# Fifteen-product block multiply over 512 tokens, in-place quarter sums, and one held PSUM bank

## The chip, the cores and the metric

The kernel runs on one core of one Trainium2 chip. The metric is device time in microseconds of one execution. The engines are named as in the profile: PE is TensorE (PEld its weight loads), DVE is VectorE, ACT is ScalarE, POOL is GpSimd, SP is the engine whose queue issues most of the transfers.

## The reference

An attention block (a linear recurrence with decay, per head) feeds a token and channel mixer. There are 4 batches, 768 tokens and 8 heads of 48, so 384 channels. All is float32.

```python
for t in range(S):                                   # attention, per batch and head
    y[t] = r[t] @ (state + outer(u * k[t], v[t]))
    state = w[t][:, None] * state + outer(k[t], v[t])
x = y, laid out as (batch, token, 384)
h = relu(x.T @ w_tok1) @ w_tok2                      # w_tok1 (768, 256), w_tok2 (256, 768)
u = x + h.T
out = u + relu(u @ w_ch1) @ w_ch2                    # w_ch1 (384, 1536), w_ch2 (1536, 384)
```

The weights arrive as 64-bit floats in their bits and are converted on the chip.

## The kernel before, in words

The attention is cut into 12 units of 256 tokens, three to a batch. While a batch is mixed, the three units of the next batch run beside it; the last batch is mixed alone. The first batch is mixed with plain matmuls, since the weights are still being converted and combined beside it.

A middle batch is written by `middle_mixing` as a list of pieces, each a cost weight and a function that issues instructions. `woven` merges lists: every piece gets the position of its middle in its list, as a fraction of the list's total weight, and the pieces are sorted by that. `strict` then makes each of PE, DVE and ACT issue its instructions in exactly the order of the merged list, so an instruction that waits holds all that stand behind it on its engine. Transfers of SP are not held to the list's order.

The mixing of a batch has these stages.

- `hidden`: the first token product, two results of 6 matmul calls each, with 384 columns. A float32 matmul call shows as two instructions in the profile.
- `back` and `turn`: six times the second token product, which DVE adds to x (L531), and three transposes into `xT`, copied by ACT (L538).
- The up projection to `z` (1536 hidden values for each token), in three segments of 256 tokens. For the batches after the first it is a block multiply with fifteen products in place of eighteen. `rights(s)` makes sums of blocks of `xT` on DVE (L569, L499), named g, h, f, e, r12, r13, r9, r0, r4, r7, r2, r10; the matching sums of `w_ch1` are made once. `thirds(s)` issues fifteen products (L582). A product is four matmul calls of 128 columns into one PSUM bank. After it come its taps: "take" is an ACT copy to `z` (L587), "plus", "minus" and "rest" are DVE adds (L590, L593, L596), and "done" is the Relu on ACT in place (L599). The numbers 14, 8, 12, 9, ... are the products' order.
- The down projection, again in three segments: `quarters(s)` splits `z` into a11, a12, a21, a22 and uses seven products p1 to p7 in place of eight. Each is two halves of three matmul calls with 192 columns (L639, L643). DVE makes four sums of quarters (L686, L687) and taps the products into the output tile `o`, of which there is one; p1 is copied by ACT to m1, and m1, u2 and u3 are running sums in SBUF (L652, L669, L675). SP stores `o` in two parts (L647).

In a middle batch each segment goes through `thirds` and then `quarters`. All middle segments use the second `z` buffer; the sums of the quarters lie in the first. Of the attention units, `ends` is a scan on DVE (L372) with a memset ahead and a reciprocal behind, `keys`, `begins` (a second scan, L380) and `queries` follow it, `tokens` transposes keys on PE, `gram`, `carry`, `before` and `after` are small PE matmuls, and `products` are three DVE operations that prepare the diagonal of a later unit. `load_rk` and its like are SP's transfers.

Eight PSUM banks: two for `carry`'s result, six in a pool `ps_m` that everything else takes in turn.

```python
keyed.append(((at + c / 2) / total, n, i, c, f))            # woven
pieces = woven(hiddens + turned[:6] + sums[:3] + ... , a0 + a1 + a2 + b0)
for s, (att, near) in enumerate(((b1, n + 1), (b2 + c0, n + 2), (c1 + c2, n + 3))):
```

Here a, b and c are the three units of the next batch: part 0 is the loads and `ends`, part 1 goes from `keys` to the first updates, part 2 from `gram` to the copies of the result.

Of the kernel before, what the change touches and what calls it, by code (L numbers as in the profile page):

```python
# [62 lines left out]
def rwkv6_then_mixer(  # L63
# [48 lines left out]

    rks = [const.tile([128, 2 * COLS], f32, name=f"rk{i}") for i in range(3)]
# [75 lines left out]
    early = [t.bitcast(u32) for t in halves]  # L189
    bits64 = [t[:, :4 * PIECE] for t in (scratch, spare, early[0])]  # L190
# [284 lines left out]
    z_sums = [halves[0][:, ts(i, HJ * 128)].rearrange("p (j t) -> p j t", j=HJ) for i in range(3)]  # L475
    w_sums = [scratch[:, ts(i, HJ * HM)].bitcast(f32).rearrange("p (j e) -> p j e", j=HJ) for i in range(3)]
    parts = halves[0][:, ds(3 * HJ * 128, 3 * HM)].rearrange("p (n e) -> p n e", n=3)
    late_sums = [t.rearrange("p q x t -> p (q x t)")[:, :HJ * 128].rearrange("p (j t) -> p j t", j=HJ) for t in ats]
    late_sums.append(starts[:, :HJ * 128].rearrange("p (j t) -> p j t", j=HJ))
    late_parts = ws[0][:, :3 * HM].rearrange("p (n e) -> p n e", n=3)  # L480
# [32 lines left out]
    def mixing(bt, x_of, out_rows):  # L513
# [5 lines left out]
        def hidden(i, c):  # L519
            if c == 0:  # L520
                sums[i] = ps_m.tile([128, DM], f32, name="h1_ps", tag="m")
            pe.matmul(sums[i], wtok1[:, c, ts(i, 128)], x_of()[:, c, :], start=(c == 0), stop=(c == C - 1))  # L522
            if c == C - 1:
                act.activation(h1[:, i, :], sums.pop(i), AF.Relu)  # L524
# [15 lines left out]
        def up(s, jt):  # L540
            if jt == 0:
                zs[s] = halves[int((bt, s) != (0, 0))].rearrange("p (j t) -> p j t", j=NJ)
            ps = ps_m.tile([128, SEG], f32, name="z_ps", tag="m")
            for m in range(DM // 128):
                pe.matmul(ps, wch1[:, m, ts(jt, 128)], xT[:, m, ts(s, SEG)],  # L545
                          start=(m == 0), stop=(m == DM // 128 - 1))
            act.activation(zs[s][:, jt, :], ps, AF.Relu)

        def rights(s):
            b = lambda k, m: xT[:, k, ds(s * SEG + m * 128, 128)]  # L550
            if not last:
                four = h1.rearrange("p i e -> p (i e)")[:, :512] if s % 2 else rights_at[:, 8 * 128:]
                eight = rights_at[:, :8 * 128]
            elif s % 2 == 0:
                near = apool.tile([128, 12 * 128], f32, name="near", bufs=1)
                four, eight = near[:, :512], near[:, 512:]
            else:
                eight, four = apool.tile([128, 8 * 128], f32, name="to_end"), apool.tile([128, 4 * 128], f32, name="kT", bufs=1)
            h, f, e, g = (four[:, ts(n, 128)] for n in range(4))
            r12, r13, r9, r0, r4, r7, r2, r10 = (eight[:, ts(n, 128)] for n in range(8))  # L560
            of = {0: r0, 1: b(0, 1), 2: r2, 3: b(0, 0), 4: r4, 5: f, 6: b(2, 1), 7: r7, 8: b(1, 0), 9: r9, 10: r10, 11: e,
                  12: r12, 13: r13, 14: g}
            hfe = four[:, :3 * 128].rearrange("p (k t) -> p k t", k=3)
            first, second = (xT[:, :, ds(s * SEG + m * 128, 128)] for m in range(2))
            sums = ((dve.tensor_add, g, b(0, 1), b(1, 1)), (dve.tensor_add, hfe, first, second), (dve.tensor_sub, r12, b(0, 0), e),
                    (dve.tensor_sub, r13, b(0, 0), b(2, 0)), (dve.tensor_add, r9, r13, g), (dve.tensor_sub, r0, b(2, 1), b(1, 0)),
                    (dve.tensor_add, r4, f, h), (dve.tensor_sub, r7, h, e), (less, r2, b(1, 1), b(2, 1)),
                    (dve.tensor_add, r10, b(1, 0), b(2, 0)))
            return of, [(0.05, lambda q=q: q[0](*q[1:])) for q in sums]  # L569

        def thirds(s, of):
            z = halves[s % 2 if last else 1].rearrange("p (j t) -> p j t", j=NJ)
            to = lambda n: z[:, ts(n // 2, JB), ts(n % 2, 128)]
            banks = {}

            def product(r, name, end):
                first = name not in banks
                if first:
                    banks[name] = bank("z_ps").rearrange("p (q t) -> p q t", q=JB)
                ps = banks[name]  # L580
                for q in range(JB):
                    pe.matmul(ps[:, q], lefts[r][:, ts(q, 128)], of[r], start=first and q == 0, stop=end and q == JB - 1,  # L582
                              skip_group_check=True)
                return ps

            def take(n, ps):
                act.copy(to(n), ps)  # L587

            def plus(n, ps):
                dve.tensor_add(to(n), to(n), ps)  # L590

            def minus(n, ps):
                dve.tensor_sub(to(n), to(n), ps)  # L593

            def rest(n, ps):
                dve.tensor_sub(to(n), ps, to(n))  # L596

            def done(n, ps):
                act.activation(to(n), to(n), AF.Relu)  # L599

            order = ((14, "x", False, [(take, 3)]), (8, "y", False, [(take, 2)]), (12, "z", False, [(take, 4)]),
                     (9, "x", False, [(plus, 2)]), (0, "y", False, [(minus, 4)]), (4, "u", False, [(take, 0)]),
                     (13, "x", True, [(minus, 0), (take, 1)]), (5, "y", False, [(take, 5)]), (6, "v", False, [(plus, 5)]),
                     (7, "z", True, [(plus, 1)]), (2, "y", True, [(plus, 3), (done, 3)]), (10, "u", True, [(rest, 2), (done, 2)]),
                     (3, "w", True, [(minus, 0), (minus, 4), (done, 0)]), (1, "q", True, [(plus, 5), (plus, 1), (done, 5), (done, 1)]),
                     (11, "v", True, [(minus, 4), (done, 4)]))

            def one(r, name, end, taps):
                ps = product(r, name, end)
                for f, n in taps:  # L610
                    f(n, ps)

            return [(0.9, lambda q=q: one(*q)) for q in order]
# [14 lines left out]
        def quarters(s):  # L628
            z = halves[s % 2 if last else 1].rearrange("p (j t) -> p j t", j=NJ)
            a11, a12, a21, a22 = (z[:, ts(j, HJ), ts(i, 128)] for i in range(2) for j in range(2))  # L630
            s1, s2, s4 = late_sums if last else z_sums
            t1, t2, t4 = w_sums
            m1, u2, u3 = ((late_parts if last else parts)[:, i] for i in range(3))
            L = {}

            def begin(a, b):
                L["q"] = ps_m.tile([128, HM], f32, name="q_ps", tag="m")
                for j in range(HJ // 2):
                    pe.matmul(L["q"], a[:, j, :], b[:, j, :], start=(j == 0), stop=False)  # L639

            def product(a, b):
                for j in range(HJ // 2, HJ):
                    pe.matmul(L["q"], a[:, j, :], b[:, j, :], start=False, stop=(j == HJ - 1))  # L643
                return L.pop("q")
# [4 lines left out]
            def p1():  # L649
                o = L["o"] = mpool.tile([128, 2, DM], f32, name="o", bufs=1)  # L650
                x = L["x"] = x_of()[:, ts(s, 2), :]
                act.copy(m1, product(a11, w11))  # L652
                dve.tensor_add(o[:, 0, :HM], x[:, 0, :HM], m1)

            def p4():
                o, x = L["o"], L["x"]
                dve.tensor_add(o[:, 1, :HM], x[:, 1, :HM], product(a22, t4))

            def p2():
                o = L["o"]  # L660
                dve.tensor_add(o[:, 0, :HM], o[:, 0, :HM], product(a12, w21))

            def p5():
                o, x = L["o"], L["x"]
                dve.tensor_add(o[:, :, HM:], x[:, :, HM:], product(s1, t1).unsqueeze(1).to_broadcast([128, 2, HM]))

            def p6():
                o = L["o"]
                dve.tensor_add(u2, m1, product(s2, t2))  # L669
                dve.tensor_add(o[:, 0, HM:], o[:, 0, HM:], u2)  # L670

            def p7():
                o = L["o"]
                both = o[:, 1].rearrange("p (n e) -> p n e", n=2)
                dve.tensor_add(u3, u2, product(a21, w12))  # L675
                dve.tensor_add(both, both, u3.unsqueeze(1).to_broadcast([128, 2, HM]))
                store(1)

            def p3():
                o = L["o"]  # L680
                dve.tensor_add(o[:, 0, HM:], o[:, 0, HM:], product(s4, w22))
                store(0)

            of = {p1: (a11, w11), p4: (a22, t4), p2: (a12, w21), p5: (s1, t1), p6: (s2, t2), p7: (a21, w12), p3: (s4, w22)}
            ps = {p: [(0.98, lambda p=p: begin(*of[p])), (0.98, p)] for p in of}
            return [*ps[p1], (0.01, lambda: dve.tensor_add(s1, a21, a22)), *ps[p4], (0.01, lambda: dve.tensor_sub(s2, s1, a11)), *ps[p2],  # L686
                    (0.01, lambda: dve.tensor_sub(a21, a11, a21)), *ps[p5], (0.01, lambda: dve.tensor_sub(s4, a12, s2)), *ps[p6], *ps[p7],  # L687
# [265 lines left out]
```

## Time and profile before

| | us |
|---|---|
| median of 3 runs | 518.55 (518.52 to 519.9) |
| the profiled execution | 518.99 |
| its span, first to last instruction | 517.3 |
| outside the span | 1.7 |
| first batch and the opening | 0 to 176.9 |
| second batch | 176.9 to 294.85 |
| third batch | 294.85 to 412.77 |
| last batch | 412.77 to 517.3 |

| engine | busy us | share | instructions |
|---|---|---|---|
| PE | 491.1 | 95% | 5794 |
| PEld | 428.4 | 83% | 5794 |
| DVE | 388.7 | 75% | 633 |
| ACT | 229.6 | 44% | 533 |

The ends of matmuls are modelled in the profile: a matmul of 192 columns shows 0.33 us, but in a stream the next one starts 0.16 us after it. So a pause of PE under about 0.2 us shows as busy, and a longer one shows shorter than it is. In a timeline a row gives the start, the length, the engine, the line and the operation; several equal instructions in a row are merged, and brackets give the idle time ahead and what ended it. "Hand-over" below is the moment at which PE could start the next matmul.

### The profile page before, as it was taken

To read this page: it belongs to the slowest core of one execution; us is meant where nothing else is said; L and a number is where in the kernel's file an instruction comes from. 1 tells how busy PE (TensorE), PEld (TensorE's weight loads), DVE (VectorE), ACT (ScalarE), POOL (GpSimd) and SP (SyncE) were. 2 spreads that over 40 slices of the span, in tenths; PEclk is the share of its full clock that TensorE was granted. 3 is DMA by queue.
4 is the path that set the end of the run, shared out by engine and by line. 5 is a ranking of instruction groups with operands and counts; after the bars stand their busy time and mean duration, and the time that the engine had idled before them with its cause. 6 is when DMAs were issued, how large, how long until landed. Compare 5 with 4: busy or idle time off the path is not lost.

```text
span 517.3 us, 13323 instructions
## 1 busy us (share of the span) xinstructions
PE 491.1 (95%) x5794; PEld 428.4 (83%) x5794; DVE 388.7 (75%) x633; ACT 229.6 (44%) x533; POOL 1.3 (0%) x10
## 2 busy tenths in 40 slices
PE   3678999999999999999999999999999999999996
PEld 2566588666789768999999868999999859999996
DVE  7999779959896878977779668987858616684653
ACT  2868665464353436434325445524335414531300
POOL 0000000000000000000000000000000000000000
PEclk9799999999999999999999999999999999999999
DMA  8856845442342442121211522100000000000000
GB/s 298 314 179 190 246 162 163 158 145 99 109 119 80 147 132 64 63 74 63 70 55 62 165 74 63 61 32 1 3 32 1 18 15 1 1 2 34 1 32 34
DMA packets 20945, 46.06 MB, mean 89 GB/s; under 512 B 2128, under 2 KB 13008, under 8 KB 20880
## 3 DMA queue, kind: packets, MB, share of 16 engines
q1 hardware_dynamic: 20736, 45.14, 27.3%
q8 instruction: 47, 0.77, 0.6%
q14 instruction: 18, 0.15, 0.1%
q10 hardware_dynamic: 144, 0.00, 0.0%
HBM read 40.41 MB, written 4.72 MB: 87 GB/s over the span
## 4 chain that ended last, share of the span: by engine, by line
PE 71%; DVE 17%; ACT 6%; issue 3%; DMA 2%; SPq 0%; DVEq 0%; ACTq 0%
PE z_ps L582 18%; PE q_ps L643 12%; PE q_ps L639 11%; PE h_ps L529 5%; PE h_ps L621 5%; PE h_ps L522 5%; PE z_ps L545 3%; PE y_ps L317 2%; PE gram L257 2%; DVE w L380 2%; PE y_ps L338 2%; PE kv_ps L303 2%; PE xT_ps L537 2%; DVE z L590 2%; DVE to_end L372 1%
## 5 line engine op out<-in xcount | busy, mean ns | idle before, releaser
L438 ACT ACTIVATE before<-state,to_end 112x48 f32<-112x48 f32 x176 | 44.5, 325 | 66.4 <-DVE state L448 62.5
L587 ACT COPY z<-z_ps 128x512 f32<-128x512 f32 x54 | 30.6, 587 | 57.4 <-PE z_ps L582 39.5
L590 DVE TENSOR_TENSOR z<-z,z_ps 128x512 f32<-128x512 f32 x54 | 36.0, 684 | 24.5 <-PE z_ps L582 15.9
L545 PE MATMUL z_ps<-xT,wch 128*128 128x256 f32 x216 | 48.1, 381 | 0.0
L599 ACT ACTIVATE z<-z 128x512 f32<-128x512 f32 x54 | 33.3, 631 | 33.1 <-DVE z L590 29.0
L545 PEld LDWEIGHTS z_ps<-xT,wch 128*128 128x128 f32 x216 | 40.6, 190 | 6.0 <-DVE wch L227 0.3
L643 PE MATMUL q_ps<-wch,z 128*128 128x192 f32 x222 | 43.3, 331 | 0.0
L639 PE MATMUL q_ps<-wch,z 128*128 128x192 f32 x222 | 42.8, 329 | 0.2
L639 PEld LDWEIGHTS q_ps<-wch,z 128*128 128x128 f32 x222 | 36.5, 190 | 0.9 <-ACT z L599 0.6
L643 PEld LDWEIGHTS q_ps<-wch,z 128*128 128x128 f32 x222 | 36.5, 190 | 0.6
L529 PE MATMUL h_ps<-h,wtok 128*128 128x384 f32 x96 | 35.1, 492 | 0.6 <-ACT h L524 0.6
L593 DVE TENSOR_TENSOR z<-z,z_ps 128x512 f32<-128x512 f32 x45 | 30.1, 685 | 6.9 <-PE z_ps L582 6.5
L621 PE MATMUL h_ps<-wch,z 128*128 128x384 f32 x96 | 33.3, 494 | 0.4 <-DVE wch L227 0.4
L522 PE MATMUL h_ps<-x,wtok 128*128 128x384 f32 x96 | 33.1, 491 | 0.0
L531 DVE TENSOR_TENSOR x<-x,h_ps 128x384 f32<-128x384 f32 x24 | 13.3, 553 | 26.1 <-PE h_ps L529 26.1
L582 PE MATMUL z_ps<-rk,wch 128*128 128x128 f32 x256 | 31.2, 275 | 0.0
L582 PEld LDWEIGHTS z_ps<-rk,wch 128*128 128x128 f32 x256 | 30.0, 192 | 0.0
L372 DVE TENSOR_TENSOR_SCAN to_end<-w,starts 112x1041 f32<-112x1041 f32 (+1 forms) x13 | 28.1, 2160 | 2.1 <-DMA w<-in_w_dram 1.7
L380 DVE TENSOR_TENSOR_SCAN w<-w,starts 112x1041 f32<-112x1041 f32 x12 | 27.9, 2322 | 0.0
L643 PE MATMUL q_ps<-scratch,z 128*128 128x192 f32 x144 | 27.7, 329 | 0.0
L639 PE MATMUL q_ps<-scratch,z 128*128 128x192 f32 x144 | 27.4, 327 | 0.0
L582 PE MATMUL z_ps<-xT,wch 128*128 128x128 f32 x216 | 27.1, 275 | 0.0
(181 smaller groups left out, 905.9 us busy)
## 6 DMA issues: line engine op xcount, KB each, us to landing
rk<-in_rk_dram SPq DMA_DIRECT2D x36, 192.0 KB, 3.8
near<-in_near_dram SPq DMA_DIRECT2D x8, 768.0 KB, 4.4
w<-in_w_dram SPq DMA_DIRECT2D x11, 520.5 KB, 4.2
vt<-in_v_dram SPq DMA_DIRECT2D x12, 384.0 KB, 4.0
out_dram<-o SPq DMA_DIRECT2D x24, 192.0 KB, 1.9
spare<-in_w_ch_dram SPq DMA_DIRECT2D x8, 512.0 KB, 4.3
scratch<-in_w_ch_dram SPq DMA_DIRECT2D x8, 512.0 KB, 4.7
rk<-in_rk_dram SPq DMA_DIRECT2D x6, 512.0 KB, 8.9
```

Of the source, the lines that this page charges most:

```text
L372: dve.tensor_tensor_scan(to, of, start, 0.0, op0=ALU.mult, op1=ALU.add)
L380: dve.tensor_tensor_scan(w_[:ROWS], w_[:ROWS], starts[:ROWS], 0.0, op0=ALU.mult, op1=ALU.add)
L438: act.mul(t[:ROWS, a], state[bt, g][:ROWS, a], by_last(c, j)[:, a:a + 1])
L522: pe.matmul(sums[i], wtok1[:, c, ts(i, 128)], x_of()[:, c, :], start=(c == 0), stop=(c == C - 1))
L529: pe.matmul(ps, wtok2[:, i, ts(c, 128)], h1[:, i, :], start=(i == 0), stop=(i == DTOK // 128 - 1))
L545: pe.matmul(ps, wch1[:, m, ts(jt, 128)], xT[:, m, ts(s, SEG)], start=(m == 0), stop=(m == DM // 128 - 1))
L582: pe.matmul(ps[:, q], lefts[r][:, ts(q, 128)], of[r], start=first and q == 0, stop=end and q == JB - 1, skip_group_check=True)
L590: dve.tensor_add(to(n), to(n), ps)
L599: act.activation(to(n), to(n), AF.Relu)
L621: pe.matmul(ps, zs[s][:, jt, ts(n, 128)], wch2[:, jt, :], start=(jt == 0), stop=(jt == NJ - 1))
L639: pe.matmul(L["q"], a[:, j, :], b[:, j, :], start=(j == 0), stop=False)
L643: pe.matmul(L["q"], a[:, j, :], b[:, j, :], start=False, stop=(j == HJ - 1))
```

## The change

The first two segments are multiplied together. With `s == 0`, `rights` and `thirds` work on 512 tokens: every block of `xT` is 256 tokens wide, and the fifteen products run twice, each with two matmul calls of 256 columns, for the first and then for the second two of each four blocks of hidden values. `z` of the first segment lies in buffer 0, of the second in buffer 1, of the third in buffer 0 again. Product 8 is issued ahead of product 14. The sum e is made alone, and three sums are written over their inputs (h, and two blocks of `xT`).

In `quarters` the sums are written over a22, a21, a11 and a12, each after the product that reads the old content. The products come in the order p4, p1, p2, p5, p6, p3, p7. p1, p6 and p7 add into one PSUM bank, tapped three times: m1, u2 and u3 are gone. That bank comes from a pool of one, `held`, which `ps_m` (now five) gives up; product bank "v" of `thirds` and the first `hidden` result of the batches after the first use it too.

A middle batch is now: hidden, back and turn; `thirds` of two segments; quarters 0; `thirds` of the third segment; quarters 1; quarters 2. The products for unit n+3 move from the third `thirds` to quarters 2. The last two turns go between the first products. In the last batch the check of the ranges (`verdict`) moves ahead of quarters 0.

```diff
+    def held(name):
+        return ps_h.tile([128, 512], f32, name=name, tag="h")
...
+    def z_of(s):
+        return halves[s % 2].rearrange("p (j t) -> p j t", j=NJ)
...
-                sums[i] = ps_m.tile([128, DM], f32, name="h1_ps", tag="m")
+                sums[i] = (held if bt and i == 0 else bank)("h1_ps")[:, :DM]
...
+            width = SEG if s == 0 else SEG // 2
...
+            b = lambda k, m: xT[:, k, ds(s * SEG + m * width, width)]
+            g, e, r12, r13, h, f = (six[:, ts(n, width)] for n in range(6))
+            r9, r0, r4 = (three[:, ts(n, width)] for n in range(3))
...
+            sums = ((dve.tensor_sub, r13, b(0, 0), b(2, 0)), (dve.tensor_add, g, b(0, 1), b(1, 1)), (dve.tensor_add, e, b(2, 0), b(2, 1)),
+                    (dve.tensor_sub, r12, b(0, 0), e), (dve.tensor_add, r9, r13, g), (dve.tensor_sub, r0, b(2, 1), b(1, 0)),
+                    (dve.tensor_add, hf, first, second), (dve.tensor_add, r4, f, h), (dve.tensor_sub, h, h, e),
+                    (less, b(1, 1), b(1, 1), b(2, 1)), (dve.tensor_add, b(2, 0), b(1, 0), b(2, 0)))
...
+            by_half = s == 0
+            count = JB // 2 if by_half else JB
+            order = ((8, "y", False, [("take", 2)]), (14, "x", False, [("take", 3)]), (12, "z", False, [("take", 4)]),
+                     (9, "x", False, [("plus", 2)]), (0, "y", False, [("minus", 4)]), (4, "u", False, [("take", 0)]),
...
+                     (1, "q", True, [("plus", 5), ("plus", 1), ("done", 5), ("done", 1)]), (11, "v", True, [("minus", 4), ("done", 4)]))
+
+            def to(n, at):
+                z = z_of(n % 2 if by_half else s)[:, ds(n // 2 * JB + at, count), :]
+                return z if by_half else z[:, :, ts(n % 2, 128)]
...
+                    banks[name] = (held if name == "v" else bank)("z_ps").rearrange("p (q t) -> p q t", q=count)
...
-                for q in range(JB):
-                    pe.matmul(ps[:, q], lefts[r][:, ts(q, 128)], of[r], start=first and q == 0, stop=end and q == JB - 1,
+                for q in range(count):
+                    pe.matmul(ps[:, q], lefts[r][:, ts(at + q, 128)], of[r], start=first and q == 0, stop=end and q == count - 1,
...
+            chain = (p1, p6, p7)
+
+            def begin(p, a, b):
+                if p in chain[1:]:
+                    L[p] = L[chain[0]]
+                else:
+                    L[p] = (held if p in chain else bank)("q_ps")[:, :HM]
+                half(0, L[p], a, b, first=p not in chain[1:])
...
+            of = {p1: (a11, w11), p4: (a22, t4), p2: (a12, w21), p5: (a22, t1), p6: (a11, t2), p7: (a21, w12), p3: (a12, w22)}
...
+            return [*ps[p4], (0.01, lambda: dve.tensor_add(a22, a21, a22)), *ps[p1], (0.01, lambda: dve.tensor_sub(a21, a11, a21)),
+                    (0.01, lambda: dve.tensor_sub(a11, a22, a11)), *ps[p2], (0.01, lambda: dve.tensor_sub(a12, a12, a11)), *ps[p5], *ps[p6],
+                    *ps[p3], *ps[p7]]
...
-    ps_g, ps_m = None, six_banks.enter_context(tc.tile_pool(name="ps_m", bufs=6, space=bass.MemoryType.PSUM))
+    ps_m, ps_h = (six_banks.enter_context(tc.tile_pool(name=name, bufs=n, space=bass.MemoryType.PSUM)) for name, n in (("ps_m", 5), ("ps_h", 1)))
...
+    def begun(turned, sums):
+        return turned[:5] + sums[:1] + turned[5:9] + sums[1:3] + turned[9:10] + sums[3:]
+
+    def with_turned(turned, ups):
+        return ups[:1] + turned[10:11] + ups[1:2] + turned[11:] + ups[2:]
...
+        pieces = woven([e for h in hiddens for e in h] + begun(turned, sums), a0 + a1 + a2 + b0)
+        ups = with_turned(turned, thirds(0, of))
+        pieces += ups[:4] + woven(ups[4:20], products_of(n + 1)) + ups[20:]
+        of, sums = rights(2)
+        pieces += woven(b1, woven(quarters(0), sums))
+        ups = thirds(2, of)
+        pieces += ups[:1] + woven(ups[1:11], products_of(n + 2)) + ups[11:]
+        pieces += woven(b2 + c0, quarters(1)) + woven(products_of(n + 3) + c1 + c2, quarters(2))
```

## The prediction

> **What bounds the kernel now.** I read the page's busy table and slices first, then the waits of TensorE in windows, then the chain for the price of a matmul, then timelines at the places the change touches.
>
> ```profile
> PE 491.1 (95%) x5794; PEld 428.4 (83%) x5794; DVE 388.7 (75%) x633; ACT 229.6 (44%) x533; POOL 1.3 (0%) x10
> PE   3678999999999999999999999999999999999996
> PEclk9799999999999999999999999999999999999999
> ```
>
> From a fifth of the span on TensorE is full, at full clock. The waits of PE in 294.85 to 412.77 us (the whole third batch) are one line:
>
> ```profile
> PE gram L257 <- DVE rk L383: 0.2, 1, 0.2
> ```
>
> So no wait of TensorE is left to take away there; a gain has to come out of its stream, and each new wait is paid in full. The chain gives the stream's prices:
>
> ```profile
> 139.06 5.38 PE z_ps L545 x24
> 145.51 2.79 PE z_ps L545 x12
> 319.98 11.61 PE z_ps L582 x104
> 412.77 7.74 PE h_ps L522 x24
> ```
>
> 5.38 - 2.79 over twelve is 215.8 ns for 256 columns, 11.61/104 is 111.6 ns for 128, 7.74/24 is 322.5 ns for 384; the chain's q_ps pieces (0.97 for six) give 162.5 for 192. Every product call is two instructions.
>
> **Stream.** In each of the last three batches 240 matmuls of 128 columns become 120 of 256: 26.79 - 25.90 = 0.9 us, three batches **-2.7**. The Trainium skill ("TensorE: Matmul & The Clock Gate", Back-to-back issue gap) puts a fixed 2.5 ns on a matmul beside its columns; 360 fewer would by that save 0.9 us in all. The rows show 2 x 111.6 - 215.8 = 7.4 ns a pair, so I take 2.7. The stream of the quarters keeps its 84 matmuls each.
>
> **Work taken off VectorE and ScalarE.** Per quarter call u2 and u3 (two ops of 0.354) and the copy m1 (0.316) go: ten calls, 7.1 us of VectorE and 3.2 of ScalarE. The sums of `rights`: 128 columns cost 0.285, 384 cost 0.555, so an estimate for 256 is 0.42; ten of these, a 0.69 and a second set of 3.3 give 8.2 instead of 9.4 us a batch. All this lies beside TensorE and is costed at nothing; without that cover it would be worth 3 us a batch. One old wait should go with it: y_ps pausing 0.6 us at 171.5 behind VectorE in the first batch. Old waits that the new order removes: product 11 to q_ps (0.29, twice) and the last batch's segment border (0.42). Together **-1.6**.
>
> **Held bank at the start of a batch.** `hidden(0, 0)` now writes the bank that p7 of the batch before has just filled, so it waits for p7's tap. The timeline at the start of the last batch (start, length, engine and line):
>
> ```profile
> 412.45 0.33 PE L643 MATMUL q_ps<-wch,z 128*128 128x192 f32 x1
> 412.61 7.90 PE L522 MATMUL h_ps<-x,wtok 128*128 128x384 f32 x24
> 412.81 0.36 DVE L681 TENSOR_TENSOR o<-o,q_ps 128x192 f32<-128x192 f32 x1 [2.28 <-PE q_ps L643]
> ```
>
> Now h_ps follows the last q_ps without a gap, and VectorE begins 0.20 after the hand-over. The new tap is 384 wide (0.558, from L676), and VectorE to TensorE takes about 0.06: 0.20 + 0.56 + 0.06 = 0.82, three times **+2.5**. All TensorE work of the batch is queued behind it.
>
> **First sums behind a scan.** The timeline at the end of `back` in the third batch:
>
> ```profile
> 316.08 1.46 PE L529 MATMUL h_ps<-h,wtok 128*128 128x384 f32 x4
> 317.58 0.56 DVE L531 TENSOR_TENSOR x<-x,h_ps 128x384 f32<-128x384 f32 x1 [1.56 <-PE h_ps L529]
> 318.20 2.33 DVE L372 TENSOR_TENSOR_SCAN to_end<-w,starts 112x1041 f32<-112x1041 f32 x1
> 320.57 0.26 DVE L373 RECIPROCAL starts<-to_end 112x16 f32<-112x16 f32 x1
> 320.74 0.42 DVE L569 TENSOR_TENSOR rk<-rk 128x128 f32<-128x128 f32 x2
> ```
>
> After the last `back` VectorE adds, scans for the next unit, and only then makes the remaining sums. Weaving weights put the scan at 0.952 of its list; the changed list has the last `back` at 0.94 and the fourth sum on at 0.978, so the scan stays in between. Before, only r4, r7, r2, r10 lay behind it, needed from the sixth product on. Now r12 does, needed by the third. r12 is done at 320.74 + 0.42 = 321.16, TensorE may go at 321.22. It hands over at 317.37 and has two products of 0.863 and two turns of 0.33 to do: free at 319.76. Wait 1.45, in the two batches with attention beside them: **+2.9**. (r9, r0 and r4 then come in 0.4 to 1.1 steps against products of 0.86: no wait. In the last batch there is no scan.)
>
> **Between the two runs of fifteen products, and after them.** Two timelines: the end of a segment's products, and the border of two segments in the last batch.
>
> ```profile
> 241.81 1.06 PE L582 MATMUL z_ps<-h,scratch 128*128 128x128 f32 x8
> 242.99 1.24 PE L639 MATMUL q_ps<-wch,z 128*128 128x192 f32 x6
> 243.50 1.83 ACT L599 ACTIVATE z<-z 128x512 f32<-128x512 f32 x3 [0.56 <-DVE z L590]
> ...
> 445.45 1.06 PE L582 MATMUL z_ps<-to_end,spare 128*128 128x128 f32 x8
> 446.14 1.54 ACT L587 COPY z<-z_ps 128x512 f32<-128x512 f32 x3
> 446.76 2.05 PE L582 MATMUL z_ps<-to_end,spare 128*128 128x128 f32 x16 [0.25 <-ACT z L587]
> ```
>
> The taps lag: product 11 hands over at 242.70, its last ScalarE "done" ends at 245.33, 2.63 later (2.17 in the other segments). Before, p1 came first and read blocks finished early. Now p4 comes first, and its second half reads blocks 9 to 11 of z; 10 and 11 are that very last "done". TensorE has the first half (0.97) and block 9 (0.33) to cover 2.17 + 0.07: 0.94 (1.40 with the longer lag). I take 1.0, three times: **+3.0**. At the border of the two runs, product 9 needs its bank copied out first. In the last batch it waits now from 445.45 + 0.89 = 446.34 to 446.76: 0.42. With 8 ahead of 14 that copy comes one copy later (+0.5) and three products are 0.09 shorter; sums woven in there now are gone (-0.4 at most). 0.6 to 1.0, I take 0.75, three times: **+2.3**.
>
> **Quarters after quarters.** Two quarter calls now follow each other, and the products of unit n+3 go into the second. I laid the queues out from the hand-over of p7 of quarters(1), t = 0, second batch. By the weights the scan of the next unit lies between p7's halves, so behind p3's tap: it begins at -1.4 and with the reciprocal ends at 1.2. p7's tap ends at 1.7; two products (0.95 each) at 3.5; p4's tap writes `o`, which must wait for the store just issued (1.9 us to land): 4.05; the third product 4.95; the a22 sum 5.8; keys (1.21) 7.0. TensorE comes to the tokens at 4 x 0.97 = 3.9: wait 3.1, with quarters and attention behind it. In the third batch there are no products; p4's tap still blocks until about 3.7, the second scan (2.32), a22, a21, a11 (0.95 each) and queries (1.22) follow, end near 10.3, and gram arrives at 8.75: 1.65. Each replaces an old 0.35. Net **+4.05**. This is the longest layout, no row shows the sequence itself: between 0, if slack absorbs it, and 6, if the store lands late; I keep the middle, because every duration has a row.
>
> **Five banks and the tail.** With five free banks the fourth `back` may wait for a copy behind a decay multiply; 0 to 0.6 in each of three batches, a gain being excluded: **+0.3**. The end now is p7's tap (0.56) instead of p3's (0.35): **+0.2**. Stores keep number and size. The in-place sums wait for the product that read the same quarter; without attention, counted from the start of p4, p4's tap and a22 (from 2.15), p1's tap, a21 and a11 end near 6.2, and p6 begins at 8 x 0.97 = 7.8: nothing.
>
> **Sum:** -2.7 - 1.6 + 2.5 + 2.9 + 3.0 + 2.3 + 4.05 + 0.3 + 0.2 = +10.95. The profiled execution took 518.99 (span 517.3 and 1.7 around it), 0.44 over the median 518.55; set on the median: 529.5.
>
> **Rivals.** *Only the border waits come* (0.20): VectorE, 3 us a batch lighter, absorbs the quarter layout and half of the product borders: -4.3 + 2.5 + 2.9 + 3.0 + 1.2 + 0.2 = +5.5, **524**. For: VectorE idles for 6 us before q_ps taps in a batch. Against: those idle pieces don't lie where the scan goes. *Faster* (0.08): the lag of VectorE is the whole of these waits, and the lighter queue has none. Then p4 waits only the bare chain 0.20 + 0.69 + 0.04 + 0.63 + 0.06 - 1.30 = 0.3, the product border and r12 nothing, and the held bank is released in the shadow: -4.3 + 1.0 + 0.2 = -3.1, **515.5**. It decides if the backlog at product 11's hand-over is under 0.3 us; the rows show about 0.6 to 1, and the scan is not removed. *Worse* (0.10): five banks starve attention (gram 2, keys 2, outputs 2, beside a quarter) or the store holds VectorE longer: over 533. The same page of the skill (What's actually happening) has an idle window of 3.4 us halve the clock: the 3.1 us wait stays under it by that rule, no row here shows a gap so late, and one half-rate window would add up to 1.7. *As worked out* (0.60), own range 527 to 532. That nothing measurable happens gets the rest, 0.02; parts of the faster and the border case end inside 0.3% (about what a measurement of this kernel can tell).
>
> **How the numbers follow.** The range 521.5 to 533 takes the border case and the bounds of the quarter layout in and leaves out the faster case and the far end. Faster by over 0.3%: 0.07; within: 0.04; slower: 0.89.
>
> **What would show it.** 5434 matmuls instead of 5794; L582's successors at 216 ns a piece; in PE's waits, h_ps on a DVE `o` add about 0.8 three times; a z_ps wait of about 1.4 on the sum r12 behind the scan, twice; q_ps on an ACT "done" about 1, three times; k_ps or gram on VectorE's rk, 3 and 1.6. VectorE's busy time should fall by about 10 us while the span grows. I am wrong if PE shows no waits in a middle batch, or if a batch takes 117 us or less instead of about 122.

## The result, and the profile after

| | us |
|---|---|
| median before, the four runs beside the changed kernel | 518.53 (518.50 to 519.9) |
| median after, 4 runs | 532.77 (531.02 to 534.03) |
| ratio | 1.0264, interval 1.0244 to 1.0284 |
| profiled execution, before and after | 518.99 and 531.02 |

The change costs 14.2 us on the medians and 12.0 between the two profiled executions; the prediction had +10.95, and 532.77 lies at the upper end of its range. The page of the changed kernel, the lines that answer to those of before:

```profile
PE 491.7 (93%) x5434; PEld 416.4 (79%) x5434; DVE 381.6 (72%) x589; ACT 226.1 (43%) x523; POOL 1.3 (0%) x10
PE   3588999899999999999997998999999899999996
PEclk9689999999999999999999999999999999999999
```

TensorE has 360 matmuls fewer and is as long busy in a longer span: its share fell from 95 to 93%. Its row of slices shows a 7 and two 8s from the middle on, where it had only 9s. VectorE and ScalarE have 7.1 and 3.5 us less work, and the kernel is slower. What became longer shows in the windows of the two middle batches, cut where `hidden` starts. The columns are the bounds, the length, busy time and number of instructions of PE, PEld, DVE, ACT and POOL, the clock, the DMA share and GB/s. Before:

```profile
176.76:294.69 117.93, 117.64 (x1440) 107.10 (x1439) 95.02 (x161) 51.65 (x124) 0.00 (x0) 1.00 0.26 82
294.69:412.61 117.92, 117.63 (x1440) 107.09 (x1439) 90.12 (x155) 51.56 (x124) 0.00 (x0) 1.00 0.12 36
```

After:

```profile
177.56:301.16 123.60, 117.47 (x1318) 102.46 (x1318) 93.09 (x147) 50.54 (x121) 0.00 (x0) 1.00 0.25 78
301.16:424.06 122.90, 117.95 (x1318) 103.03 (x1318) 87.82 (x140) 50.50 (x121) 0.00 (x0) 1.00 0.11 34
```

A middle batch stood still for 0.3 us and now stands still for 6.1 and 5.0; the clock is full in all four rows. TensorE's waits in the changed kernel (us in total, times, longest) name every stop. Second batch, with the start of the third (177 to 303):

```profile
PE k_ps L294 <- DVE rk L384: 2.9, 1, 2.9
PE h_ps L524 <- DVE starts L375: 1.3, 2, 0.6
PE z_ps L601 <- DVE rk L569: 1.2, 1, 1.2
PE q_ps L629 <- ACT z L589: 0.8, 1, 0.8
PE z_ps L601 <- ACT z L587: 0.5, 1, 0.5
```

Third batch, with the start of the last (303 to 427):

```profile
PE z_ps L601 <- DVE rk L569: 1.6, 1, 1.6
PE gram L264 <- DVE rk L390: 1.3, 1, 1.3
PE q_ps L629 <- ACT z L589: 0.8, 1, 0.8
PE h_ps L524 <- DVE o L659: 0.6, 1, 0.6
PE z_ps L601 <- ACT z L587: 0.5, 1, 0.5
```

Before, the third batch had one line of 0.2. (The shown idle time leaves out about 0.2 of a pause, since the ends of matmuls are modelled; below, "with its hidden part" adds it.) The wait on "DVE starts L375" is the held bank: p7's tap L659 releases it, and the memset right behind the tap is only the later event.

Four places in the second batch, in the timeline of the changed kernel: the scan behind the last `back`, and the sum r12; the border of the two runs of fifteen products; the start of quarters 0; and the passage from quarters 1 to quarters 2:

```profile
201.17 2.33 DVE L379 TENSOR_TENSOR_SCAN to_end<-w,starts 112x1041 f32<-112x1041 f32 x1
203.70 0.36 DVE L569 TENSOR_TENSOR rk<-xT,rk 128x256 f32<-128x256 f32 x1
204.12 1.13 PE L601 MATMUL z_ps<-rk,spare 128*128 128x256 f32 x4 [1.23 <-DVE rk L569]
...
217.64 1.54 ACT L587 COPY z<-z_ps 128x512 f32<-128x512 f32 x3
218.75 1.99 PE L601 MATMUL z_ps<-h,spare 128*128 128x256 f32 x8 [0.55 <-ACT z L587]
...
229.60 1.82 ACT L589 ACTIVATE z<-z 128x512 f32<-128x512 f32 x3 [0.57 <-DVE z L591]
231.48 0.92 PE L629 MATMUL q_ps<-scratch,z 128*128 128x192 f32 x4 [0.80 <-ACT z L589]
...
278.80 0.49 DVE L659 TENSOR_TENSOR o<-o,q_ps 128x384 f32<-128x384 f32 x1
279.21 0.94 DVE L407 TENSOR_TENSOR near<-near 128x768 f32<-128x768 f32 x1
280.19 0.96 DVE L409 TENSOR_TENSOR near<-near,u_rows 128x768 f32<-128x768 f32 x1
281.29 0.35 DVE L637 TENSOR_TENSOR o<-x,q_ps 128x192 f32<-128x192 f32 x1
281.56 0.94 DVE L412 TENSOR_REDUCE sums<-near 128x16 f32<-128x768 f32 x1
282.42 0.95 DVE L677 TENSOR_TENSOR z<-z 128x768 f32<-128x768 f32 x1
283.29 1.22 DVE L384 TENSOR_TENSOR rk<-rk,to_end 112x1024 f32<-112x1024 f32 x1
284.56 1.09 PE L294 MATMUL k_ps<-ident,rk 128*128 128x128 f32 x8 [2.91 <-DVE rk L384]
```

VectorE issues in order, so r12 comes only after the 2.33 us scan, and TensorE starts its product 0.06 after r12. At 218.75 the ninth product's bank still has to be copied out: this is the border. At 231.48 the second half of p4 starts when the last of three Relus is through. In the last eight rows, three product operations, a tap and a sum of quarters stand in VectorE's queue ahead of the keys, and the tokens on TensorE wait 2.91 for them. Every wait in the two lists ends on something in VectorE's or ScalarE's queue, with VectorE busy for only 72% of the span. The 72% are an average: from 280 to 284 us, ahead of the tokens, it was busy for 3.82 of 4 us. One of them is lengthened by a transfer: in the third batch, ahead of gram, p4's tap waits 0.88 us for the store of `o`, the only output tile, with the second scan behind it (no run gave `o` a second buffer).

### The profile page after: what moved, and what is told of

Read it like the earlier page. It is cut to its first block, busy times and chain, and to the rows that moved or that the text cites. A ratio compares the mean times of both kernels' runs of the same rounds, so it can differ in the third digit from the quotient of the medians.

```text
span 529.3 us, 12544 instructions
## 1 busy us (share of the span) xinstructions
PE 491.7 (93%) x5434; PEld 416.4 (79%) x5434; DVE 381.6 (72%) x589; ACT 226.1 (43%) x523; POOL 1.3 (0%) x10
## 4 chain that ended last, share of the span: by engine, by line
PE 67%; DVE 17%; ACT 6%; DMA 6%; issue 3%; SPq 1%; DVEq 0%
PE q_ps L629 23%; PE z_ps L601 15%; PE h_ps L615 6%; PE h_ps L531 5%; PE h_ps L524 5%; PE z_ps L547 3%; DVE to_end L379 3%; PE y_ps L324 2%; DMA w<-in_w_dram 2%; PE gram L264 2%; ACT z L589 2%; PE kv_ps L310 2%; PE y_ps L345 2%; DVE z L593 2%; DMA rk<-in_rk_dram 2%
## 5 line engine op out<-in xcount | busy, mean ns | idle before, releaser
L629 PE MATMUL q_ps<-wch,z 128*128 128x192 f32 x480 | 84.6, 329 | 0.0
L629 PEld LDWEIGHTS q_ps<-wch,z 128*128 128x128 f32 x480 | 78.1, 190 | 0.7
L629 PE MATMUL q_ps<-scratch,z 128*128 128x192 f32 x360 | 64.7, 329 | 2.1 <-ACT z L589 2.1
L629 PEld LDWEIGHTS q_ps<-scratch,z 128*128 128x128 f32 x360 | 58.6, 190 | 3.6 <-ACT z L589 3.0
L547 PEld LDWEIGHTS z_ps<-xT,wch 128*128 128x128 f32 x216 | 40.6, 190 | 5.9 <-DVE wch L234 0.3
L601 PE MATMUL z_ps<-xT,wch 128*128 128x256 f32 (+1 forms) x240 | 42.2, 327 | 0.0
L601 PEld LDWEIGHTS z_ps<-xT,wch 128*128 128x128 f32 x240 | 36.7, 191 | 3.1
L524 PEld LDWEIGHTS h_ps<-x,wtok 128*128 128x128 f32 x96 | 17.4, 190 | 13.2 <-DVE starts L375 1.9
L615 PEld LDWEIGHTS h_ps<-wch,z 128*128 128x128 f32 x96 | 17.6, 190 | 12.7 <-ACT z L549 2.0
L295 ACT COPY kT<-k_ps 128x512 f32<-128x512 f32 x24 | 13.1, 585 | 25.7 <-PE k_ps L294 25.7
```

What stands on the lines that cost most here:

```text
L601: pe.matmul(ps[:, q], lefts[r][:, ts(at + q, 128)], of[r], start=first and q == 0, stop=end and q == count - 1, skip_group_check=True)
L615: pe.matmul(ps, zs[s][:, jt, ts(n, 128)], wch2[:, jt, :], start=(jt == 0), stop=(jt == NJ - 1))
L629: pe.matmul(ps, a[:, j, :], b[:, j, :], start=first and j == 0, stop=last and j == HJ - 1, skip_group_check=True)
```

## The experiments

Theory: the time is the sum of these waits, each set by the order of the in-order queues and not by the amount of work. Rivals: that taking one away only moves it on; that the 256-column products are slower or gain nothing by themselves; that a lower clock carries part of it. All edits are made to the changed kernel. Ratios are to the kernel before, on the same chip.

### e1: `hidden` gets a bank of the pool

```diff
-                sums[i] = (held if bt and i == 0 else bank)("h1_ps")[:, :DM]
+                sums[i] = bank("h1_ps")[:, :DM]
```

> The changed kernel, but the first hidden result of a batch takes a bank of the pool of five instead of the held one. Theory (it waits for p7's tap of the held bank): the 0.65 us idle ahead of h_ps at the start of batches 2, 3 and 4 goes; with the 0.2 us that the modelled end hides, 0.85 each, 2.5 us in all: about 530.3 where the changed kernel had 532.8, 1.2% over... 2.3% above the kernel before. Rival (something else at a batch's start is late, such as the copies of the attention's result): the idle stays, 532.8. Rival (the pool of five becomes too small): the idle goes but new ones of 0.5 us or more appear in hidden and back, gain under 1 us.

Measured: 532.2 (529.07 to 533.41), ratio 1.0256 [1.0216, 1.0296]. The interval covers the changed kernel's 1.0264, so the reading is made on the profiles, both at full clock from 32 us on: 529.07 against 531.02, -1.95. The stop at the start is gone in all three batches. In the second batch a new one stands behind it:

```profile
181.25 1.06 PE L294 MATMUL k_ps<-ident,rk 128*128 128x128 f32 x8 [0.59 <-PE h_ps L524]
```

The tokens want a bank of the five and the first `hidden` result, now one of them, has to be finished first. So the mechanism holds at its price (2.5), less 0.6 that the smaller pool takes back.

### e2: the scan ahead of the last `back`

```diff
-        pieces = woven([...] + begun(turned, sums), a0 + a1 + a2 + b0)
+        pieces = woven([...] + begun(turned, sums), a0 + a1 + a2[:-4] + b0 + a2[-4:])
```

> The changed kernel, with the scan of the next unit placed ahead of the last attention piece and the copies of its result, so that it lies before the last back on VectorE and not between its add and the sums. Theory (r12 is late only because the scan is issued ahead of it): the waits of product 12 (1.23 and 1.64 us idle, 1.4 and 1.8 with the hidden part) go, about -3.2 us, 529.6. Rival (VectorE is short of time there whatever the order): the wait moves to the last turn or to product 9, gain under 1.5 us.

Measured: 531.72 (530.39 to 532.74), ratio 1.0236 [1.0197, 1.0276]. The r12 waits are gone from the trace; in their place TensorE waits 0.32 twice ahead of product 14, on the last `back` itself:

```profile
203.28 1.13 PE L601 MATMUL z_ps<-rk,wch 128*128 128x256 f32 x4 [0.32 <-DVE x L533]
```

From the start of a batch to the border took 40.34 instead of 41.19 us, and 40.84 instead of 42.11 in the third: -0.85 and -1.27, together -2.1 where -3.2 was expected. The profiled execution is no shorter (531.77 against 531.02): its first batch, which the edit does not touch, ended 1.2 later (its first matmul already came 1.4 later), and a stretch of lower clock, shown in the last section, cost 1.7. The step is confirmed in kind; a part of the wait moves on, since the scan is only nearer the front of the same queue.

### e3: product 11 ahead of product 1

```diff
-                     (1, "q", True, [("plus", 5), ("plus", 1), ("done", 5), ("done", 1)]), (11, "v", True, [("minus", 4), ("done", 4)]))
+                     (11, "v", True, [("minus", 4), ("done", 4)]), (1, "q", True, [("plus", 5), ("plus", 1), ("done", 5), ("done", 1)]))
```

> The changed kernel with the last two of the fifteen products exchanged: 11 before 1. Theory (p4's second half waits for the very last Relu, behind four taps and two Relus of product 1): the three waits of q_ps on L589 (0.80, 0.81, 0.47 us idle, with the hidden part 3.0 together on first estimate, 2.7 by these rows) go, nothing takes their place: about -2.5 us, 530.2. Rival (VectorE's backlog is the cause, not the position): p4 or p1 waits as long as before, gain under 0.7 us.

Measured: 532.12 (529.46 to 535.54), ratio 1.0257 [1.0195, 1.032]. The waits of q_ps on ACT are gone from all three batches, so it was the last Relu that p4 waited for. The border's wait grew by 0.2 (0.74, 0.75 and 0.67 instead of 0.55, 0.55 and 0.47). From the border to the tokens of the second batch took 1.0 us less, from the border to gram of the third 0.84 less, and the last batch up to its last hand-over 0.54 less. Less the 0.2 that the border adds in the two middle batches, that is -2.0 where -2.5 was expected. The profiled execution (531.18) does not show it: it holds a stretch of lower clock worth 1.45, and it ended 0.7 later after its last matmul. The medians don't resolve a gain of this size: the four runs are 6 us apart.

### e4: the products of the later units back into the up projections

```diff
-        pieces += ups[:4] + woven(ups[4:20], products_of(n + 1)) + ups[20:]
+        pieces += ups[:4] + woven(ups[4:16], products_of(n + 1)) + woven(ups[16:28], products_of(n + 2)) + ups[28:]
...
-        pieces += ups[:1] + woven(ups[1:11], products_of(n + 2)) + ups[11:]
-        pieces += woven(b2 + c0, quarters(1)) + woven(products_of(n + 3) + c1 + c2, quarters(2))
+        pieces += ups[:1] + woven(ups[1:11], products_of(n + 3)) + ups[11:]
+        pieces += woven(b2 + c0, quarters(1)) + woven(c1 + c2, quarters(2))
```

The tile `sums` has three buffers in it.

> The changed kernel with the products of unit n+3 taken out of quarters 2 again: those of n+1 and n+2 lie in the first two segments' products, those of n+3 in the third's (with a third buffer for their sums). Theory (keys is late because of these three operations of 0.95 us): the tokens wait of 2.9 us idle in batch 2 falls to under 0.5 and the gram wait of about 1.3 us, as in batch 3, comes instead: about -1.7 us, 531. Rival (the store of the single output tile holds VectorE, and keys with it): tokens still waits over 1.5 us. A side of it: if the spread of the changed kernel's times (531.0 to 534.0) comes from the clock falling after that 2.9 us pause, the times of this kernel lie closer together.

Measured: 531.76 (531.49 to 532.64), ratio 1.0244 [1.0209, 1.0279]; profiled 531.73 at full clock, no faster than the changed kernel's 531.02. Two of its waits in the second batch:

```profile
PE gram L264 <- DVE rk L390: 1.3, 1, 1.3
...
PE z_ps L601 <- ACT z L587: 1.1, 1, 1.1
```

The tokens' 2.9 is gone, and gram waits 1.34 in its place, on the queries behind the second scan: without the products the second batch behaves as the third already did. The products, put among the up projections, lengthen the wait at the border from 0.55 to 1.07 and add 0.34 on a tap. The second batch is 0.45 shorter (123.15), the third 1.1 longer (124.03). So the products, and not the store of `o`, held the tokens in the second batch, but the 1.7 us that were expected from it did not come: here the rival that a wait only moves on is right.

### e5: the same products in 128-column matmuls

```diff
-                    pe.matmul(ps[:, q], lefts[r][:, ts(at + q, 128)], of[r], start=first and q == 0, ...)
+                    for m in range(JB // count):
+                        pe.matmul(ps[:, q, ts(m, 128)], lefts[r][:, ts(at + q, 128)], of[r][:, ts(m, 128)], ...)
```

> The changed kernel, but each 256-column matmul of the products is issued as two of 128 columns into the same bank (360 more matmuls, as before the change). It measures the one gain of the change. Theory (111.6 against 215.8 ns, 7.4 ns a pair): TensorE's stream is 2.7 us longer; in the profile a run of fifteen products takes 13.4 us instead of 12.95. In the total some of it is given back, since the border wait (0.55 us idle) and the q_ps wait (0.8) shrink by about 0.1 each: profiled time about 533, with the same clock. Rival (a matmul has a fixed 2.5 ns beside its columns): 0.9 us longer, 13.1 us a run.

Measured: 532.71 (532.53 to 534.3), ratio 1.0276 [1.025, 1.0302]; profiled 532.73 against 531.02, both at full clock: +1.7. The twelve products from the border on, whose rows run without a pause in either kernel, began at 218.93 and ended with q_ps at 229.75, 10.82 us; in the changed kernel from 218.75 to 229.21, 10.46. The first two rows are of e5, the third of the changed kernel, whose border row stands above:

```profile
218.93 2.05 PE L602 MATMUL z_ps<-h,spare 128*128 128x128 f32 x16 [0.33 <-ACT z L587]
229.75 1.47 PE L630 MATMUL q_ps<-scratch,z 128*128 128x192 f32 x8
...
229.21 1.46 PE L629 MATMUL q_ps<-scratch,z 128*128 128x192 f32 x8
```

The 0.36 over 48 pairs of matmuls are 7.5 ns a pair, 2.7 us in the kernel. Of this 0.9 came back as shorter waits (the border 0.33 instead of 0.55, q_ps 0.74 and 0.41 instead of 0.80 and 0.47), as slower products give the taps time. So the wide products do gain, and at the price of the rows in the prediction (7.4 ns a pair) rather than at 2.5 ns. Those rows also show where the rest comes from: 162.5, 215.8 and 322.5 ns for 192, 256 and 384 columns lie on one line, which has 2.5 ns left at no columns; at 128 columns it would give 109.2, and the row has 111.6. The fixed 2.5 ns are there, and the 128-column matmul takes another 2.4; why it does, no run here shows.

### e6: all four edits of e1 to e4

> The four edits of the experiments before this one together (h_ps in the pool, scan earlier, 11 before 1, products back). Theory (the waits are separate causes and add up): from the profiled 531.0 the held bank takes 1.9, the scan 2.1, the exchange 2.5, the products about 0, and with no pause of TensorE near 3 us left the clock stays full, so the median comes down by another 1.7: about 524.5 profiled and median. Left: the border waits (1 us idle now, as the products lie before them), gram 1.3 twice. Rival (one shortage of VectorE moves from place to place): 528 or more.

Measured: 526.32 (525.14 to 527.36), ratio 1.0144 [1.0118, 1.017]: 6.4 us off the changed kernel, far outside its interval, and the first step that the medians resolve. Its waits from 177 to 420:

```profile
PE gram L264 <- DVE rk L390: 2.9, 2, 1.6
PE z_ps L601 <- ACT z L587: 2.5, 2, 1.3
PE z_ps L601 <- DVE x L533: 0.6, 2, 0.3
PE k_ps L294 <- PE h_ps L524: 0.6, 1, 0.6
```

Left in the middle batches are 1.3 at each border, gram's 1.33 and 1.57, twice 0.3 behind `back`, and the tokens' 0.6 that e1 had. Its profiled execution (526.13) holds a stretch of lower clock, shown below, worth some 1.7 us; without it the trace gives 524.4, as expected. That the clock would stay full was not borne out.

### e7: the pieces put in a new order

To e6: the scan of the next unit's `b0` seven pieces before the end of the attention list; `c0`, with its scan, among the third segment's products, and its keys in quarters 1; the products of n+2 between pieces 20 and 28; and pieces of the two runs of fifteen exchanged at their border. The last of these in code:

```diff
-        return ups[:1] + turned[10:11] + ups[1:2] + turned[11:] + ups[2:]
+        return ups[:1] + turned[10:11] + ups[1:2] + turned[11:] + ups[2:13] + ups[15:16] + ups[13:14] + ups[16:17] + ups[14:15] + ups[17:]
```

> Built on the four edits: the first two products of the second run go between the last ones of the first, so that their copies are not queued behind all of its Relus; the next unit's scan moves from quarters 1 into the third segment's products, its keys into quarters 1; the products of n+2 lie later. Theory (the change's gain is 2.7 us of stream and about 1.6 us of old waits, and every loss is a wait of one order of issue): no pause of TensorE over 0.5 us is left in a middle batch, which takes about 116.5 us against 117.9 before the change; total about 514.5, 0.8% faster than before. Rival (with five banks and one held the waits cannot all be removed): at or above 518.5.

Measured: 517.0 (515.37 to 519.18), ratio 0.996 [0.9946, 0.9973]. The two middle batches took 116.52 and 116.88 us, as expected, with one wait of 0.6 and one of 0.7 in them; the total is 2.5 above the expected 514.5. Moving `b0` and `c0` whole also moved their transfers of r and k; what that did to the data stands in the next expectation.

### e8: the same order, with the transfers where they were

```diff
-        pieces = woven([...] + begun(turned, sums), a0 + a1 + a2[:-7] + b0 + a2[-7:])
+        pieces = woven([...] + begun(turned, sums), a0 + a1 + a2[:-7] + b0[1:] + a2[-7:-4] + b0[:1] + a2[-4:])
...
-        pieces += ups[:1] + woven(ups[1:11], products_of(n + 3) + c0) + ups[11:]
-        pieces += woven(b2 + c1[:1], quarters(1)) + woven(c1[1:] + c2, quarters(2))
+        pieces += ups[:1] + woven(ups[1:11], products_of(n + 3) + c0[1:]) + ups[11:]
+        pieces += woven(b2 + c0[:1] + c1[:1], quarters(1)) + woven(c1[1:] + c2, quarters(2))
```

> The rearranged kernel with the transfers of r and k issued where they were, behind the last use of the buffers that they fill (in the rearranged kernel before this one they came earlier, over r and k still in use, so that part of its attention was made from another unit's data; its instructions were the same). Theory (the order alone makes the time): like that one, 516 to 517, 0.3 to 0.5% faster than the kernel before the change, no pause of TensorE over 0.8 us in a middle batch. Rival (the earlier transfers were what removed waits): some wait on a transfer or on keys comes back, 518.5 or more.

Measured: 515.74 (515.53 to 516.63), ratio 0.9944 [0.9929, 0.9959]: faster than the kernel before by 2.7 us of medians in the same group of runs, and faster than the changed one by 17. Its page, its waits from 177 to 412, and its windows of the two batches, cut where `hidden` starts:

```profile
PE 486.8 (95%) x5434; PEld 414.6 (81%) x5434; DVE 381.7 (74%) x589; ACT 225.7 (44%) x523; POOL 1.3 (0%) x10
```

```profile
PE z_ps L601 <- ACT z L587: 0.7, 1, 0.7
PE k_ps L294 <- PE h_ps L524: 0.6, 1, 0.6
```

```profile
176.69:293.21 116.52, 115.93 (x1320) 102.08 (x1320) 92.68 (x147) 50.24 (x121) 0.00 (x0) 1.00 0.27 83
293.21:410.09 116.88, 116.16 (x1319) 102.25 (x1319) 87.94 (x141) 50.37 (x121) 0.00 (x0) 1.00 0.12 37
```

The matmuls are the same 5434, VectorE and ScalarE do the same work (381.7 and 225.7), and of the stops of some 5 and 6 us a batch there are 0.6 and 0.7 left, the same as in e7, so the earlier transfers had removed none of them. This is the direct test of the theory: none of the change's arithmetic cost time; the places of a few pieces in the queues and the bank lent to `hidden` did. The batches are 1.4 and 1.0 us shorter than before the change.

### e9: the changed kernel once more

> The changed kernel itself, for the spread of its times. Theory (the clock of TensorE sometimes falls after one of its long pauses, for about 1.7 us of lost work each time): times in steps, from about 531 with none over 532.7 to 534.4; the profiled execution either shows full clock after 100 us and takes about 531, or a stretch of 4 us under 0.8 behind the tokens pause or the gram pause, and is that much longer. Rival (the spread comes from the opening, where weights are loaded and converted): the start of the second batch, 177.6 us in the profiled one, moves by as much as the total, with full clock behind it.

Measured: 532.52 (530.91 to 533.9), ratio 1.027 [1.025, 1.029]; the profiled execution, 530.91, has the waits shown above and full clock from 32 us on, and its second batch starts at 177.45. The result stands, and again the profiled execution is the lowest of its runs; what sets the spread stays open (last section).

## Why the prediction held, and where it was off

The sign, the mechanism and the size were right: lost by the order of the queues, not by the work. Step by step, measured waits with their hidden part:

| step | predicted | measured |
|---|---|---|
| wide products | -2.7 | -2.7 (e5) |
| held bank at a batch's start | 3 x 0.82 | 3 x 0.85 |
| r12 behind the scan | 2 x 1.45 | 1.43 and 1.84 |
| border of the two runs | 3 x 0.75 | 0.75, 0.75, 0.67 |
| second half of p4 | 3 x 1.0 | 1.0, 1.0, 0.67 |
| tokens behind the products | 3.1 | 3.1 |
| gram behind the queries | 1.65 | 1.5 |
| longer last tap | +0.2 | +0.35 |
| first batch's old wait on y_ps | -0.6 | the wait went, a new stop took more: net +0.5 |
| five banks, last three batches | +0.3 | no wait of TensorE on record there |

**Quarters after quarters** was called the longest layout, with no row for the sequence. It came as laid out. From the hand-over of p7 at 277.59 the reciprocal ended at 1.3 (1.2 predicted), p7's tap at 1.7 (1.7), p4's tap at 4.1 (4.05), the a22 sum at 5.8 (5.8) and the keys at 6.9 (7.0). Laying a queue out row by row was worth it: this was the largest term.

**The total** of the middle batches by the same terms is +5.7 for the second, and it measured +5.67 (123.60 against 117.93). The third has +4.98, where the terms give 4.2: 0.4 of the difference is r12, the rest has no row that I can name. The last batch up to its last hand-over has +0.2 where the terms give 0.5.

**What failed** is the term for the old waits of the first batch. The y_ps wait was to go with VectorE's lighter queue and to shorten that batch by 0.6. It did go, but a new stop of the down projection took more than was gained. Two waits from 60 to 177 us, the first before and the second after:

```profile
PE y_ps L317 <- ACT before L438: 0.6, 1, 0.6
...
PE h_ps L615 <- ACT z L549: 1.8, 1, 1.8
```

Its bank waits for a copy that stands behind a conversion on ScalarE, the kind of price that the five banks were given 0.3 for in the other batches; no run gave the pool its sixth bank back, so that the five banks are its cause is argued from the row. Two later waits of that batch, 0.4 and the 0.6 of y_ps, are gone. From the first matmul of the down projection (95.50 before, 94.95 after) to the second batch took 81.26 us before and 82.61 after: 1.35 more, of which 0.85 are the held bank and 0.5 the stop less the two waits.

The start of the second batch hides this: it lies at 176.76 before and 177.56 after, as if only the held bank had come (and at 176.63 in e1, without the held bank). The profiled execution after had an earlier opening, with its first matmul at 8.30 us instead of 9.02. In e2, with the changed kernel's instructions up to there, it was at 9.66, so a difference of this size can be chance.

The profiled executions differ by 12.03 and the sum said 10.95; of the 1.1 between them, about 0.6 is this term less the earlier opening, 0.75 the third batch, and the last batch takes 0.2 off.

**The median** was forecast at 529.5 and came 3.3 above, 0.2 inside the range. Only 1.1 of that is the sum. The other 2.2 come from where the profiled execution lies among its runs, 0.44 above the median before and 1.75 below it after, and the working has no term for that. That the median still lay inside the range is in part luck.

**The rivals.** The faster case (515.5) is what e8 reached (515.74), but only with an order that puts the scan elsewhere: the lag it wished away had to be taken out by hand. The border case fell with the layout of the quarters, and of the worse case's starved attention nothing came beyond the two waits that had a term. The clock window, which the prediction kept for its worst case, is not excluded by the runs, as the last section shows.

## What to carry to other kernels

When every engine issues in order and one is at 95%, price a change by what stands ahead of each producer in its queue when the full engine arrives; a shorter list of operations on a half-idle engine says nothing. Write the queue out with a row for each operation: of the waits priced so, only r12 in the third batch and p4's in the last were off by more than 0.2 us. And when a change that shortens the full engine's stream comes out slower, list that engine's new waits and move their producers together: singly, the edits gave too little for the medians to resolve or moved the wait on, and in the right order they gave 17 us.

## What the runs showed of the hardware

TensorE's clock fell during or shortly after pauses of 1.6 to 2.9 us, in three of the kept profiles. Windows of 4 us around the tokens' pause, columns as above with the clock ahead of the DMA share. In e2, which pauses there for 2.9 us as the changed kernel does:

```profile
284.00:288.00 4.00, 3.09 (x15) 3.09 (x16) 4.00 (x4) 2.05 (x6) 0.00 (x0) 0.72 0.51 187
```

In the changed kernel:

```profile
280.00:284.00 4.00, 1.65 (x11) 1.36 (x9) 3.82 (x6) 0.00 (x0) 0.00 (x0) 1.00 0.21 61
284.00:288.00 4.00, 3.44 (x52) 3.22 (x53) 3.96 (x5) 1.98 (x6) 0.00 (x0) 1.00 0.49 188
```

The same tokens, twelve q_ps and kv_ps took 5.73 us in e2 and 4.05 in the changed kernel: 1.7 lost to the clock. e3 lost 1.45 at this place, and e6 about 1.7 after gram's pause of 1.57:

```profile
407.00:411.00 4.00, 3.50 (x72) 3.44 (x73) 2.33 (x6) 2.02 (x8) 0.00 (x0) 0.73 0.02 4
```

The Trainium skill ("TensorE: Matmul & The Clock Gate", What's actually happening) asks for an idle window of 3.4 us; here a pause of about half of that was followed by the fall, and the measurement decides.

In windows of a quarter of a us each of the three falls is a stretch of 3.4 us at a clock of 0.50, so 1.7 us of work are lost where TensorE is full. In e2 and e6 it began 0.8 and 1.4 us after TensorE had started again, in e3 0.4 before. From 40 us to the last matmul the eleven kept profiles show no other fall; but the changed kernel, e1, e5 and e9 have the same pause of 2.9 us, and no fall. What decides between the two was not measured.

Whether such falls make the spread of the changed kernel's times (530.9 to 534.0 in nine runs) is open. A loss of 1.7 us would fit the distance between its profiled execution and its median. But e7, which has no wait over 0.7 us in its middle batches, spreads as widely (515.4 to 519.2 in eighteen runs), the kernel before goes from 518.2 to 521.5, and in e2 the second batch started 1.2 us later than in the changed kernel with the same instructions ahead of it, behind a first matmul at 9.66 instead of 8.30. The mean clock of a run does not tell these apart, as it takes in the opening too: the profiled executions of the changed kernel and of e9 have 0.987 and 0.990, both with full clock from 32 us on.
